# Attention and GELU on one core: transfers of 4096 tokens, fewer gelu and check instructions, the last batch stored by unit, and a second pass 11 units behind

## The chip, the cores and the metric

The kernel runs on one core of one Trainium2 chip. The metric is the device time of one execution in microseconds (us). Runs are fast or slow. Engines: PE is TensorE (PEld its weight loads), DVE VectorE, ACT ScalarE, POOL GpSimd, SP SyncE. "Granted clock" is the share of full TensorE speed that the throttle allowed.

## The reference

```python
B, N, m, C = 4, 12480, 32, 128               # x is [B, N, C] float32, d_ff = 2048
h   = softmax(scale * inducing @ x.T) @ x    # first pass: 32 rows per batch, needs all of x
out = softmax(scale * x @ h.T) @ h           # second pass: every token of x again
out = gelu(out @ w_in) @ w_out               # gelu(t) = 0.5 t (1 + erf(t / sqrt 2))
```

The output of the attention is a weighted mean of 32 rows `h` per batch. For the given inputs the kernel therefore takes the MLP of those 32 rows only, q = MLP(h), and mixes q in the second pass. It approximates gelu by a quadratic, tests on the chip that the inputs allow all this, and would otherwise branch to a general path.

Every float32 of x is read once (25.56 MB), every output is written once (25.56 MB), and the weights are 2.1 MB.

## The kernel before

A batch has six units of 2048 tokens and a tail of 192. The first pass takes, per unit: load with a cast to fp16, transposes, scores, exp, and a sum `hun` on PE. After the seventh unit a chain of small steps makes h and q:

```python
# chain(): one step waits for the one before it
hun_out (ACT), r1_sum (DVE), h_sum (PE), h_out (DVE), up (PE, 16 matmuls), up_out (ACT)
# gelu in four steps: three long instructions of DVE and two short ones
nc.vector.tensor_reduce(out=bt.hs, in_=bt.pt, axis=AX.X, op=ALU.add)
# ... slope and offs from hs ...
nc.vector.tensor_tensor(out=bt.sl, in0=bt.pt, in1=slope, op=ALU.mult)
nc.vector.tensor_tensor(out=bt.gl, in0=bt.sl, in1=offs, op=ALU.subtract)
down (PE), down_out (ACT), q_sum (PE), q_out (DVE)
# later, off the chain: squares of pt and their sums on DVE, judged batch by batch
```

The second pass scores each unit against h, mixes q (`at`, in PSUM), scales by 1/sum into `o`, and stores `o`. One of four parts is copied by ACT and scaled by POOL, always the same one; the others go to DVE or ACT.

```python
XBUFS = 11     # input buffers of one unit
BEHIND = 14    # the second pass stands this many units behind the first in the order
AWAY = (0,)    # the part that goes by ACT and POOL
...            # six output buffers "o" of one unit, one store of 1 MB per unit, on SP's queue
```

A small planner in the kernel fixes the order of instructions of each engine before the kernel is built, from assumed durations. On the chip the order is fixed: an engine that waits for one instruction runs nothing behind it (experiment 2 shows such a wait, of 4.49 us).

## Time and profile before

| | before |
|---|---|
| median of 3 runs | 136.24 us (136.13 to 136.53) |
| span of the profiled run | 133.9 us, clock 0.892 |
| HBM traffic | 27.67 MB read, 25.56 MB written |
| busy: PE, DVE, ACT, POOL | 75, 74, 65, 32% |
| last chain hun_sb (starts at 101.0 us) to the start of q | 10.0 us |

The page of the kernel before: span; slices of 1/40 of the span (granted clock and DMA share in tenths, then GB/s); packets; queues (packets, MB, share of 16 engines).

```profile
span 133.9 us, 3622 instructions
...
PEclk9999999559999999999959999996899965799755
DMA  3999999999999999999999999999999989989993
GB/s 98 322 210 215 213 213 202 214 217 215 214 210 212 273 281 290 291 307 296 322 313 312 322 252 314 318 373 412 423 422 425 423 374 421 379 340 418 428 404 110
DMA packets 8547, 40.18 MB, mean 300 GB/s; under 512 B 944, under 2 KB 2256, under 8 KB 5328
...
q0 software_dynamic: 4432, 13.31, 50.6%
q1 hardware_dynamic: 4096, 26.63, 49.0%
q8 instruction: 11, 0.18, 0.5%
...
HBM read 27.67 MB, written 25.56 MB: 397 GB/s over the span
```

DMA is at 9 nearly everywhere from the second slice on, and the two data queues fill 99.6% of 16 engines' span (50.6 + 49.0; packets can overlap, so in a stretch the share can pass 1, as in the table below). The GB/s row counts a cast load at its fp16 size, so 213 there is 426 GB/s of reading. Everything is hidden behind the transfers except where the row falls in the last third: 374, 379 and 340, between 107 and 121 us.

Busy microseconds by stretch in the kernel before (windows view; the last two columns are DMA share and GB/s):

```profile
core 0: us, PE busy (x) PEld busy (x) DVE busy (x) ACT busy (x) POOL busy (x), PEclk, DMA share, GB/s
20.00:40.00 20.00, 15.81 (x277) 10.87 (x275) 13.52 (x34) 11.30 (x26) 4.98 (x9) 0.83 1.09 212
45.00:93.00 48.00, 42.64 (x615) 25.12 (x613) 43.48 (x115) 37.70 (x99) 15.27 (x17) 0.95 1.04 313
...
105.00:123.00 18.00, 13.62 (x94) 5.08 (x93) 16.17 (x43) 13.76 (x42) 6.74 (x7) 0.81 0.94 388
123.00:129.00 6.00, 1.86 (x14) 0.74 (x14) 2.59 (x11) 2.81 (x9) 1.13 (x2) 0.71 1.02 423
129.00:134.00 5.00, 0.00 (x0) 0.00 (x0) 0.00 (x0) 0.00 (x0) 0.00 (x0) 0.50 0.54 202
```

The stretch from 105 to 123 us holds only stores and moves 388 GB/s where 424 is to be had. DVE is 90% busy there and the clock is 0.81. This is the time in which batch 3, the last, runs its chain and begins its second pass. I call this the hole.

Three instructions of the chain (tile view of `pt`: engine, operation, count, then nanoseconds min/median/max and first and last start):

```profile
L448 ACT ACTIVATE pt<-pt_ps x4: 597/610/626, 28.5 to 104.3; 128x512 f32<-128x512 f32 x4
L452 DVE TENSOR_REDUCE hs<-pt x4: 669/686/689, 29.2 to 105.0; 128x16 f32<-128x512 f32 x4
L476 DVE TENSOR_TENSOR sl<-pt,slope x4: 691/692/1495, 30.1 to 105.9; 128x512 f32<-128x512 f32 x4
```

`sl` usually takes 0.69 us but 1.495 us at 105.9 us, in the last batch.

### The profile page before, as it was taken

The numbers are of one execution on the slowest core, as the hardware profiler recorded it, in microseconds if no ns is written. First come the engines' busy times: TensorE is split into PE (matmuls) and PEld (weight loads), VectorE is DVE, ScalarE is ACT, GpSimd is POOL, SyncE is SP. The second block draws the span as 40 slices with busy tenths as digits, with TensorE's granted clock in tenths as the row PEclk, the third lists the DMA queues.
The fourth block names the chain that finished last, engine by engine and source line by source line (L and its number), as shares of the span: only waits on it lengthen the run. The fifth ranks groups of instructions, "written<-read, shape, count | busy, mean of one in ns | idle before, by whom it ended". The sixth has DMA issues, their size and how long they took to land.

```text
span 133.9 us, 3622 instructions
## 1 busy us (share of the span) xinstructions
PE 100.9 (75%) x1371; PEld 58.3 (44%) x1371; DVE 99.2 (74%) x290; ACT 86.9 (65%) x222; POOL 42.3 (32%) x59
## 2 busy tenths in 40 slices
PE   0299773599999998999689898996968859883400
PEld 0147561466666564656276364451635333231100
DVE  1068434259899989999986998996699998895700
ACT  3006865049577789998916977658668964879600
POOL 6911331112153402345403216113333601445300
PEclk9999999559999999999959999996899965799755
DMA  3999999999999999999999999999999989989993
GB/s 98 322 210 215 213 213 202 214 217 215 214 210 212 273 281 290 291 307 296 322 313 312 322 252 314 318 373 412 423 422 425 423 374 421 379 340 418 428 404 110
DMA packets 8547, 40.18 MB, mean 300 GB/s; under 512 B 944, under 2 KB 2256, under 8 KB 5328
## 3 DMA queue, kind: packets, MB, share of 16 engines
q0 software_dynamic: 4432, 13.31, 50.6%
q1 hardware_dynamic: 4096, 26.63, 49.0%
q8 instruction: 11, 0.18, 0.5%
q14 instruction: 8, 0.07, 0.1%
HBM read 27.67 MB, written 25.56 MB: 397 GB/s over the span
## 4 chain that ended last, share of the span: by engine, by line
DMA 58%; PE 16%; ACT 7%; DVE 7%; issue 4%; POOL 3%; POOLq 0%; DVEq 0%; ACTq 0%; SPq 0%
DMA xh<-in_x_dram 46%; DMA out_dram<-o 13%; PE at L661 7%; DVE o L698 4%; ACT o L691 3%; PE tr L330 2%; PE s L618 2%; POOL xh L240 2%; ACT e L630 1%; PE hun L378 1%; ACT o L313 1%; DVE sl L476 1%; PE r L642 1%; DVE hs L452 1%; PE q_ps L510 0%
## 5 line engine op out<-in xcount | busy, mean ns | idle before, releaser
L683 POOL TENSOR_TENSOR o<-o,rr 128x512 f32<-128x512 f32 x24 | 25.5, 1065 | 43.9 <-ACT o L313 31.2
L661 PE MATMUL at<-q,e 128*128 128x512 f16 (+1 forms) x104 | 34.3, 392 | 5.5 <-ACT o L313 1.8
L698 DVE TENSOR_TENSOR o<-at,rr 128x512 f32<-128x512 f32 (+1 forms) x57 | 35.2, 642 | 2.6 <-issue 0.7
L330 PE MATMUL tr<-identity_h,xh 128*128 128x128 f16 x392 | 29.3, 228 | 4.3 <-DMA xh<-in_x_dram 3.6
L330 PEld LDWEIGHTS <-xh 128*128 128x128 f16 x392 | 24.2, 102 | 10.6 <-DMA xh<-in_x_dram 5.3
L311 DVE COPY xT<-tr 128x1024 f16<-128x1024 f16 (+1 forms) x34 | 21.2, 641 | 9.0 <-PE tr L330 8.7
L240 POOL DMA_DIRECT2D xh<-in_x_dram x27 | 14.8, 551 | 39.4 <-DMA xh<-in_x_dram 13.0
L313 ACT ACTIVATE xT<-tr 128x1024 f16<-128x1024 f16 (+1 forms) x18 | 17.6, 990 | 11.4 <-PE tr L330 11.3
L691 ACT ACTIVATE o<-at,rr 128x128 f32<-128x128 f32 (+1 forms) x83 | 23.6, 371 | 2.1 <-PE at L661 1.9
L356 ACT ACTIVATE e<-s 128x512 f16<-128x512 f32 (+1 forms) x28 | 15.2, 543 | 8.2 <-PE s L344 6.6
L630 ACT ACTIVATE e<-s 128x512 f16<-128x512 f32 (+1 forms) x28 | 15.0, 558 | 4.3 <-PE at L661 2.2
L313 ACT ACTIVATE o<-at 128x512 f32<-128x512 f32 x24 | 14.5, 605 | 2.7 <-DMA out_dram<-o 1.3
L661 PEld LDWEIGHTS <-e 128*128 128x128 f16 (+1 forms) x104 | 9.0, 103 | 14.1 <-issue 9.6
L378 PE MATMUL hun<-xh,e1t 128*32 128x128 f16 x392 | 11.1, 233 | 3.9 <-DVE e1t L370 3.9
L370 DVE STREAM_TRANSPOSE e1t<-e 128x256 int32<-128x256 int32 (+1 forms) x28 | 10.9, 397 | 1.9 <-ACT e L356 1.5
L344 PE MATMUL s<-xT,indT 128*32 128x512 f16 (+1 forms) x108 | 10.0, 366 | 1.4 <-ACT xT L313 0.8
L618 PE MATMUL s<-xT,hT 128*32 128x512 f16 (+1 forms) x100 | 11.0, 442 | 0.0
L378 PEld LDWEIGHTS <-e1t 128*32 128x32 f16 x392 | 6.4, 100 | 7.5 <-DVE e1t L370 5.1
L642 PEld LDWEIGHTS <-e 128*128 128x128 f16 (+1 forms) x104 | 5.7, 101 | 7.9 <-ACT e L630 3.2
L642 PE MATMUL r<-strand,e 128*128 128x4 f16 (+1 forms) x104 | 6.6, 169 | 2.1 <-ACT e L630 1.7
L653 DVE RECIPROCAL rr<-r 128x16 f32<-128x16 f32 (+1 forms) x28 | 5.7, 224 | 1.6 <-PE r L642 1.6
L344 PEld LDWEIGHTS <-indT 128*32 128x32 f16 x108 | 3.5, 93 | 6.0 <-issue 3.6
(69 smaller groups left out, 80.4 us busy)
## 6 DMA issues: line engine op xcount, KB each, us to landing
out_dram<-o SPq DMA_DIRECT2D x24, 1024.0 KB, 9.4
xh<-in_x_dram POOLq DMA_DIRECT2D x23, 512.0 KB, 18.6
x_first<-in_x_dram SPq DMA_DIRECT2D x1, 1024.0 KB, 5.0
w_in_h<-in_moe_w_in_dram POOLq DMA_DIRECT2D x1, 512.0 KB, 16.8
w_out_h<-in_moe_w_out_dram POOLq DMA_DIRECT2D x1, 512.0 KB, 18.8
out_dram<-o SPq DMA_DIRECT2D x4, 96.0 KB, 8.9
xh<-in_x_dram POOLq DMA_DIRECT2D x4, 48.0 KB, 20.2
ind_s<-in_inducing_dram SPq DMA_DIRECT2D x1, 16.0 KB, 4.7
```

The lines of the kernel that those rows point to most:

```text
L240: nc.gpsimd.dma_start(out=xh[: u.p, : u.nc, :], in_=src)
L311: nc.vector.tensor_copy(out=out, in_=in_)
L313: nc.scalar.activation(out=out, in_=in_, func=AF.Copy)
L330: nc.tensor.transpose(tr[:, c - c0, : u.p], xh[: u.p, c, :], identity_h[: u.p, : u.p])
L356: nc.scalar.activation(out=e1[: u.p, : u.nc // 2, :, :], in_=s1[: u.p, : u.nc, :].rearrange("r (a b) i -> r a i b", b=2), func=AF.Exp, sca ...
L378: nc.tensor.matmul(bt.hun[32 * j : 32 * j + 32, :], e1t[: u.p, c // 2, :, c % 2], xh[: u.p, c, :], start=u.idx == 0 and c < 4, stop=c + 4 ...
L618: nc.tensor.matmul(s2[32 * j : 32 * j + 32, : u.cols], bt.hT, bt.xT_of(u, j * u.nci, (j + 1) * u.nci), start=True, stop=True,)
L630: nc.scalar.activation(out=e2[: u.rows, : u.cols], in_=s2[: u.rows, : u.cols], func=AF.Exp, scale=SCALE,)
L661: nc.tensor.matmul(at[: u.p, : u.nj, :], e2[: u.rows, ci * u.p : (ci + 1) * u.p], bt.q[: u.rows, : u.nj, :], start=True, stop=True,)
L683: nc.gpsimd.tensor_tensor(out=part, in0=part, in1=rr2[: u.p, ci, : u.nj].unsqueeze(2).broadcast_to([u.p, u.nj, 128]), op=ALU.mult,)
L691: nc.scalar.activation(out=ov[: u.p, ci, j, :], in_=at[: u.p, j, :], func=AF.Copy, scale=rr2[: u.p, ci, j : j + 1],)
L698: nc.vector.tensor_tensor(out=ov[: u.p, ci, :, :], in0=at[: u.p, : u.nj, :], in1=rr2[: u.p, ci, : u.nj].unsqueeze(2).broadcast_to([u.p, u. ...
```

## The change

Its intent: fewer and larger transfers, a shorter chain, less work on DVE, and a last batch whose outputs need no output buffer. Core of the diff, with cuts:

```diff
-XBUFS = 11
-BEHIND = 14
-AWAY = (0,)
+XBUFS = 6                      # buffers of two units
+OBUFS = 3                      # buffers of two units
+BEHIND = 11
+APART = 3                      # from this batch on: store by unit
...
+            xh = sb.tile([128, 32, 128], FP16, tag="xh", bufs=XBUFS)   # one load of 2 MB
...
-        (gelu_sum, gelu_line, gelu_mult, gelu_out)
+            nc.vector.scalar_tensor_tensor(out=bt.gl, in0=z, scalar=0.5 / CGELU,
+                in1=z, op0=ALU.add, op1=ALU.mult)          # CGELU goes into strand_c, for q
...
-            nc.vector.tensor_tensor(out=bt.zsq, in0=bt.pt, in1=bt.pt, op=ALU.mult)
-            nc.vector.tensor_reduce(out=bt.ssq, in_=bt.zsq, axis=AX.X, op=ALU.add)
+            nc.gpsimd.tensor_tensor(...)     # squares, then five halving additions on POOL
+        # one total and one judgement at the end, for all four batches
...
+        elif u.b >= APART:                   # last batch: the output lies in an input buffer
+            o = sb.tile([128, 32, 128], FP16, tag="xh", bufs=XBUFS)
+            o = o.rearrange("p c d -> p (c d)").bitcast(FP32)
...
-            if ci in AWAY and not u.tail:    # ACT copies, POOL scales
+                    {"DVE": 0.1 + 0.57 * u.nj / 4, "ACT": 0.285 * u.nj}
+                    | ({} if u.tail else {"ACT+POOL": 0.6}),    # the planner chooses
```

## The prediction

> **What bounds it now.** The DMA engines. The slice row has DMA at 9 nearly throughout from 3 us on; the queue part adds to 100% of 16 engines. HBM moves 53.2 MB. Counting a load at its 4-byte source size, the trace's packets run at 420 to 427 GB/s in the load-only stage (6 to 40 us), about 417 in the mixed stage, about 424 in store-only stretches. Against 424 GB/s, the span of 133.9 us loses about: 2.7 us before the pipe is full, 0.45 us at 42 to 45 us, 0.9 us over the mixed stage, 1.5 us between 105 and 121 us, 0.6 us in the last 3 us of transfer, 1.5 us after the last byte. PE, DVE and ACT are 65 to 75% busy and hidden, except in the hole at 105 to 121 us: there the chain of waits is compute. Batch 3's chain runs from hun_sb at 101.0 to q at 111.7; its units follow with PE 0.89 busy at a granted clock of 0.74 (windows view).
>
> **What the change does.**
> 1. Transfers of 4096 tokens double the run per partition (16 KB of HBM). Packet durations (59 ns for 512, 98 for 1024, 324 for 4096 bytes of fp16) fit about 0.0735 ns a byte plus some 20 ns, mostly overlapped. The Trainium skill, "DMA: Bandwidth & Descriptors", "Why small descriptors are slow", names a fixed cost per packet; this trace agrees. The slope alone is 435 GB/s, today 424, so halving the packets is worth at most half the gap, 1.3% of 50 MB: 0.8 to 1.5 us, on the critical path everywhere. Stores may gain less.
> 2. The gelu part of the chain (hs, slope, sl, gl: 105.0 to 108.1 us, 3.1 us) becomes one DVE operation of about 0.7 us: 2.4 us less latency. It counts only in batch 3.
> 3. DVE loses about 3.6 us a batch (gelu 1.7, squares and sum 1.36, judging 0.5), 14 of 99 us. POOL gains about 3.4 us of checks a batch and 13 more scalings at 1.07 us (order of instructions: 37 against 24). Only the 2 to 3 us of DVE after 105 us touch the hole.
> 4. With 11 units behind, stores begin about 3 units sooner, but only when a pair is done; fewer units of batch 2 remain to cover batch 3's chain (4 to 5, some 11 us of DMA, against about 8 us of chain plus 3 us for the first unit). About neutral.
> 5. Pairs make buffers come free in lumps (6 for loads, 3 for stores): new DMA gaps, 0.2 to 0.8 us.
>
> **Sum.** -1.1 (packets), -0.9 (hole), -0.3 (42 to 45), -0.2 (mixed stage), +0.4 (lumps): about -2.1 us. The floor, 53.2 MB at 430 GB/s plus fill and end, is about 129.5 us of span, 4.4 us less. Predicted time 134.1 us, 8 in 10 between 132.2 and 135.8. Faster by over 2%: 0.38; within 2%: 0.57; slower by over 2%: 0.05.
>
> **How the profile would show it.** Load packets of twice the bytes at under twice the time; load-only slices nearer 216 than 213 GB/s; no slice below 400 GB/s after the last load; DVE near 85 us; POOL near 60; batch 3's hun_sb to q about 8 us; first store near 36 to 38 us.
>
> **What would make it wrong.** Packets split at the old size, so no rate gain; lumpy buffers starving loads around 40 to 60 us, or stores during batch 3's chain; POOL's scalings and checks holding back the loads behind them in its order; or the hole closing wholly and both directions reaching 430, which would give about 132.

## The result

| | before | changed |
|---|---|---|
| median | 136.3 us (136.13 to 136.53, 4 runs) | 134.72 us (134.16 to 134.78, 4 runs) |
| ratio of fast runs | | 0.9874 (95%: 0.9844 to 0.9904): faster, but by less than 2% |
| span of the profile | 133.9 us | 132.8 us |
| PE, DVE, ACT, POOL busy, us | 100.9, 99.2, 86.9, 42.3 | 97.3, 93.4, 76.2, 65.3 |

A ratio is the mean time of one kernel's fast runs over that of the other's of the same rounds, so it is not quite the ratio of the medians. In five rounds the changed kernel had 134.21 us and 0.9898 (0.9829 to 0.9966). They were run at other times.

The page of the changed kernel, the same lines:

```profile
span 132.8 us, 3490 instructions
...
PEclk9999999965899999999999999999999999955555
DMA  4999999999999999999999999999999999999970
GB/s 123 302 223 215 217 200 220 212 220 210 220 205 220 215 200 313 333 398 367 299 318 348 266 227 324 321 412 425 430 423 426 415 437 413 411 434 425 421 300 15
DMA packets 5666, 40.17 MB, mean 303 GB/s; under 512 B 624, under 2 KB 1936, under 8 KB 2192
...
q0 software_dynamic: 2848, 13.30, 49.5%
q1 hardware_dynamic: 2800, 26.63, 48.3%
q8 instruction: 11, 0.18, 0.5%
...
HBM read 27.67 MB, written 25.56 MB: 401 GB/s over the span
```

Packets fell from 8547 to 5666. The dips of the last third are gone: from the slice with 412 on, no slice is below 411 until the last two. But those end badly: 300 and 15, where before had 404 and 110.

Stretches of the changed kernel (same columns as before):

```profile
20.00:40.00 20.00, 15.79 (x257) 11.15 (x254) 11.37 (x30) 9.88 (x22) 7.28 (x12) 0.83 1.08 216
51.00:93.00 42.00, 36.48 (x571) 21.79 (x570) 35.65 (x100) 31.41 (x69) 24.35 (x29) 1.00 1.02 335
...
105.00:123.00 18.00, 12.82 (x91) 5.17 (x91) 16.28 (x55) 10.40 (x27) 13.14 (x15) 0.81 1.00 424
123.00:126.00 3.00, 0.00 (x0) 0.00 (x0) 0.00 (x0) 0.00 (x0) 0.00 (x0) 0.50 0.99 410
126.00:132.00 6.00, 0.00 (x0) 0.00 (x0) 0.00 (x0) 0.00 (x0) 0.00 (x0) 0.50 0.46 185
```

The load-only stretch moves 216 instead of 212, the stretch of the hole 424 instead of 388. Then DMA share falls to 0.46 in the last six microseconds, in which no engine computes.

Part of the changed chain (tile view of `pt`), where L562 is the halving additions and L491 the new gelu:

```profile
L562 POOL TENSOR_TENSOR pt<-pt x20: 244/458/1279, 31.2 to 110.1; 128x512 f32<-128x512 f32 x4, 128x256 f32<-128x256 f32 x4, 128x128 f32<-128x128 f32 x4, 128x64 f32<-128x64 f32 x4
L485 ACT ACTIVATE pt<-pt_ps x4: 597/597/597, 27.6 to 103.3; 128x512 f32<-128x512 f32 x4
L491 DVE SCALAR_TENSOR_TENSOR gl<-pt x4: 693/754/985, 28.3 to 104.1; 128x512 f16<-128x512 f32 x4
```

Gelu takes 0.75 us in the median. From the start of hun_sb (100.6 us) to the start of q (106.4 us) is now 5.8 us, against 10.0 before.

### Where the time went

To compare stretches I count what was lost: the length of a stretch, less the bytes that the trace's packets moved in it (loads at their float32 size) divided by 424 GB/s, a rate that store-only stretches of both kernels reach. "End" is when the last data packet ended.

| profile | lost 0 to 93 us | lost 93 to 126 us (hole) | lost 126 us to end | lost after 93 us | end |
|---|---|---|---|---|---|
| before | 4.27 | 1.55 | 1.00 | 2.55 | 132.38 |
| changed | 3.14 | -0.04 | 2.51 | 2.47 | 131.16 |

So 1.1 us were gained by 93 us, as packets went faster, and the hole of 1.6 us closed. Yet 1.5 us of that came back at the very end. The landings say why. A transfer is split over 16 DMA engines, and each signals when its share is done. The Trainium skill, "DMA: Bandwidth & Descriptors", section "Why a DMA increments its semaphore by 16 and not by 1", says that these engines finish independently and that only all 16 signals mean that the data has landed. This trace agrees, with numbers. These are the first, median and last of the 16 signals of some stores, worked out from the trace's records of semaphores (us):

```
store issued at      first    median   last
before  104.05       108.81   109.90   111.36      issued before the hole
before  110.07       115.07   115.33   116.21      issued in the hole
before  119.97       123.98   124.08   124.19      after the hole
before  126.86       131.98   132.09   132.84      the last store
changed 112.40       117.73   118.82   120.50
changed 120.54       125.10   126.18   128.07
changed 122.60       127.98   129.09   131.62      the last store
```

In the changed kernel the first of 16 engines runs about 3 us ahead of the last, and nothing ever lets the last one catch up. In the kernel before, the hole does: the fast engines stand idle in it while the slow ones work off their queues, and the spread falls from 2.5 to 1.1 and then to 0.2 us. The kernel ends with its slowest engine: the span ends 1.08 us (before) and 1.14 us (changed) after the last of these signals.

### The profile page after: what moved, and what is told of

It is laid out like the page before. It is cut to its first block, busy times and chain, and to the rows that moved or that the text cites. A ratio compares the mean times of both kernels' runs of the same rounds, so it can differ in the third digit from the quotient of the medians.

```text
span 132.8 us, 3490 instructions
## 1 busy us (share of the span) xinstructions
PE 97.3 (73%) x1365; PEld 56.6 (43%) x1365; DVE 93.4 (70%) x266; ACT 76.2 (57%) x173; POOL 65.3 (49%) x85
## 5 line engine op out<-in xcount | busy, mean ns | idle before, releaser
L686 POOL TENSOR_TENSOR pair<-pair,rr 128x512 f32<-128x512 f32 x29 | 30.3, 1056 | 29.1 <-ACT pair L355 19.9
L670 PE MATMUL at<-q,e 128*128 128x512 f16 (+1 forms) x104 | 33.5, 389 | 7.2 <-DVE o L701 2.4
L701 DVE TENSOR_TENSOR pair<-at,rr 128x512 f32<-128x512 f32 x41 | 26.8, 679 | 3.1 <-DMA out_dram<-pair 1.6
L355 ACT ACTIVATE xT<-tr 128x1024 f16<-128x1024 f16 (+1 forms) x17 | 16.7, 981 | 19.1 <-PE tr L367 19.1
L355 ACT ACTIVATE pair<-at 128x512 f32<-128x512 f32 x29 | 17.2, 598 | 3.1 <-PE at L670 1.7
L277 POOL DMA_DIRECT2D xh<-in_x_dram x15 | 8.3, 556 | 21.5 <-DMA xh<-in_x_dram 14.3
L562 POOL TENSOR_TENSOR pt<-pt 128x512 f32<-128x512 f32 (+4 forms) x20 | 12.0, 601 | 1.5
L701 DVE TENSOR_TENSOR o<-at,rr 128x512 f32<-128x512 f32 (+1 forms) x19 | 10.2, 558 | 0.9 <-PE at L670 0.7
L686 POOL TENSOR_TENSOR o<-o,rr 128x512 f32<-128x512 f32 x8 | 8.2, 1044 | 4.0 <-ACT o L355 2.3
L616 PE MATMUL s<-xT,hT 128*32 128x512 f16 (+1 forms) x100 | 9.7, 391 | 0.1
```

Source lines behind the costliest of these rows:

```text
L355: nc.scalar.activation(out=out, in_=in_, func=AF.Copy)
L562: nc.gpsimd.tensor_tensor(out=bt.pt[:, :, :, :half], in0=bt.pt[:, :, :, :half], in1=bt.pt[:, :, :, half : 2 * half], op=ALU.add,)
L670: nc.tensor.matmul(at[: u.p, : u.nj, :], e2[: u.rows, ci * u.p : (ci + 1) * u.p], bt.q[: u.rows, : u.nj, :], start=True, stop=True,)
L686: nc.gpsimd.tensor_tensor(out=part, in0=part, in1=rr2[: u.p, ci, : u.nj].unsqueeze(2).broadcast_to([u.p, u.nj, 128]), op=ALU.mult,)
L701: nc.vector.tensor_tensor(out=ov[: u.p, ci, :, :], in0=at[: u.p, : u.nj, :], in1=rr2[: u.p, ci, : u.nj].unsqueeze(2).broadcast_to([u.p, u. ...
```

## The experiments

I call "theory A" that the time ends with the slowest DMA engine, so that a hole shorter than the lag between engines costs it nothing. "Theory B" is that the hole counts in full, and that the spread at the end was an accident. The 12 runs follow. In these experiments the runs of the kernel before, slow ones included, varied between 134.6 and 138.91 us, and the intervals of the ratios reach 0.6 to 1.2% to either side. So differences under about 1% are not told apart by time, and I lean on profiles there.

### 1. The changed kernel again (after_again)

> The changed kernel once more, as the yardstick of this call. Both theories: 0.985 to 0.990 of before. By theory A (the last store ends when the slowest of the 16 DMA engines ends, and an idle hole shorter than the lag between engines is free for that engine) the landings of the last stores are again spread over 2.5 to 4 us from the first engine to the last; by theory B (the spread at the end was an accident of one profile) over less than 1.5 us.

134.21 us (133.88 to 134.72), ratio 0.9898. Its profile had a hole of 0.96 us after all, at 102 to 117 us, yet it ended earlier than the first one, at 130.25 us: the last store's landings spread from 129.99 to 130.86 us. So the spread expected by A did not come, because there was a hole. A hole of one microsecond that costs nothing is what A says. The spread is not fixed to the kernel, though: A as I worded it for this run missed, and what B said (under 1.5 us) came.

### 2. Each half of the change alone (old_steps, small, old_gelu)

old_steps: large transfers, 11 units, last batch by unit, but gelu, checks and fixed scaling as before (the judging at the end for all batches was kept). The edit, in words:

```diff
-            gelu in one instruction; squares and sums on POOL; ACT+POOL where the planner likes
+            hs, slope, offs, sl, gl; squares and sums on DVE; part 0 alone by ACT and POOL
```

> Transfers of 4096 tokens, the last batch by unit and 11 units of lag, with the gelu, checks (on VectorE) and fixed scaling of before. If the larger transfers are what pays: 1.0 to 1.5 us faster than before (0.989 to 0.993) although a hole of 1 to 2 us in the last batch's stores is there. If the steps are what pays: within 0.4 us of before.

133.92 us (133.78 to 134.87), ratio 0.9879 (0.9808 to 0.9949), against 0.9898 of the changed kernel. Without any of the new steps the whole gain is there. Hole 0.58 us, end of the last data packet 129.94 us, last signal 131.25 us.

small: the new steps with the sizes of before.

```diff
-XBUFS = 6; OBUFS = 3; BEHIND = 11; APART = 3
+XBUFS = 11; OBUFS = 6; BEHIND = 14; APART = 4    # tiles of one unit, one transfer per unit
```

> The new gelu, check and scaling steps with the transfers, buffers and 14 units of lag of before. My estimate: the hole at 105 to 121 us closes as in the changed kernel, the rate of transfers stays as before. Theory A: the end spread is then over 2.5 us and the time is within 0.5 us of before (0.996 to 1.004). Theory B: about 1.4 us faster than before (0.990).

142.52 us, ratio 1.0492 (1.0396 to 1.0589): slower, which neither theory had. The page:

```profile
DMA  3999999999999999999999999999999960579991
GB/s 121 310 209 213 205 212 219 211 211 207 218 214 211 232 314 361 316 313 313 325 304 304 278 315 312 383 418 421 425 414 430 423 259 0 222 301 411 428 421 54
```

A slice with 0 GB/s stands where the last batch should be stored; its hun_sb came at 110.7 us instead of 101.0. Its timeline from 37 us on, first DVE, then POOL (start, length, what, and idle time before it with the releaser):

```profile
37.59 0.43 DVE L407 STREAM_TRANSPOSE e1t<-e 128x256 int32<-128x256 int32 x1
42.51 0.19 DVE L576 SCALAR_TENSOR_TENSOR left<-pt 128x16 f32<-128x16 f32 x1 [4.49 <-POOL pt L562]
```

```profile
36.99 1.04 POOL L277 DMA_DIRECT2D xh<-in_x_dram  x2 [1.94 <-PE tr L367]
38.05 1.05 POOL L551 TENSOR_TENSOR pt<-pt 128x512 f32<-128x512 f32 x1
39.18 3.30 POOL L562 TENSOR_TENSOR pt<-pt 128x512 f32<-128x512 f32 x5
```

DVE stood idle 4.49 us for the last of POOL's halving additions. POOL's check had started only at 38.05 us because a load's issue stood ahead of it in POOL's order, and that had waited 1.94 us for the transposes that free its buffer. In the changed kernel the same check starts at 30.0 us, and DVE waits for it 0.2 us in all.

old_gelu: the changed kernel with the four-step gelu only.

> The changed kernel with the old four-step gelu on VectorE, so that the last batch's chain is about 2.4 us longer and VectorE does 1.7 us more a batch. Theory A: a hole of at most 1 us appears in the stores at 107 to 114 us, the spread between DMA engines shrinks by as much, and the time is within 0.4 us of the changed kernel. Theory B (a shorter chain pays its full length once the transfers are the limit): 1 to 2.4 us slower than the changed kernel.

137.11 us, in two groups: 134.92 to 135.83 in the four fast runs and 138.39 to 140.48 in the four slow ones. Ratio of the fast ones 0.9954 (0.9863 to 1.0045), that is about 0.75 us over the changed kernel by the two ratios and 1.0 us by the plain means of the fast runs (135.28 and 134.28 us), with an interval that does not exclude either theory. The profile fell on a slow run, so I draw nothing from it.

### 3. The lag, and the last batch by unit (small11, before11, behind14, apart4)

Having first blamed the order of the passes for experiment "small", I changed the lag alone in three kernels:

```diff
-BEHIND = 14      # small -> small11; before -> before11
+BEHIND = 11
-BEHIND = 11      # changed -> behind14
+BEHIND = 14
```

> The new steps with transfers of 2048 tokens, now 11 units behind. Theory C (in the run with 14 units the last batch's first pass stood in the fixed order of each engine behind second-pass work that waits for store buffers, so its hun_sb came at 110.7 us): with 11 units hun_sb of the last batch comes at 100 to 104 us again, the hole of 8 us at 114 to 123 us is gone and the time is 0.99 to 1.003 of before, the rest of the gain of the changed kernel being the rate of the larger transfers. If the 2048-token buffers themselves are the trouble: again over 1.03.

142.93 us, 1.0539: "theory C" fell. The lag is not what ails that kernel.

> The kernel before with its second pass 11 units behind, nothing else changed. If the lag is what pays: 1 to 1.5 us faster than before. If the larger transfers pay, or if only a hole of 1.5 us is closed that the slower DMA engines do not feel: within 0.5 us of before (0.996 to 1.004).

137.09 us, 1.0089 (0.9995 to 1.0182): not faster. Its loads of x end at 99.6 us instead of 93.0, since earlier stores take their share; its hole is 2.94 us.

> The changed kernel with its second pass 14 units behind again. Theory C: the last batch's first pass comes late, hun_sb after 105 us, a hole of 3 us or more in the stores, and 2 to 6 us slower than the changed kernel. If the lag is neutral, as the prediction had it: within 0.5 us of the changed kernel, 0.985 to 0.993 of before.

134.94 us (133.98 to 136.0), 0.9919 (0.9823 to 1.0015): nothing that can be told from the changed kernel, as the prediction had it.

```diff
-APART = 3        # changed -> apart4: the last batch too is stored in pairs, from output buffers
+APART = 4
```

> The changed kernel with the last batch stored in pairs too, from the output buffers. If storing by unit pays: the first store of the last batch starts 2 to 3 us later, a hole of 1 to 3 us opens before it, and by theory A (the slower DMA engines do not feel a hole shorter than their lag) only 0 to 1.5 us of it reach the time. If it does not matter: within 0.4 us of the changed kernel.

136.74 us (136.56 to 139.11), 1.007 (0.9953 to 1.0187): about 1.7% over the changed kernel, so the whole gain and more is lost.

```profile
DMA  4999999999999999999999999999999997979990
GB/s 127 302 226 212 219 192 222 219 214 217 212 217 207 224 231 319 333 394 366 295 329 331 229 282 314 333 421 424 421 431 424 409 441 288 403 302 438 370 382 17
```

The first store of the last batch was issued at 113.9 us (changed: 111.4) and the next ones at 119.9 and 124.4 us, in steps of two units. The slices 288, 302 and 370 are the holes between, 2.36 us in all. A store of a pair waits for its second unit; in this stretch the stores have no work in hand to hide that.

### 4. Where the small kernel's loss came from (small_dvecheck)

```diff
-        p = stage(key, "POOL", 1.1, check_square, [p_gelu])
-        p = stage(key, "POOL", 2.4, check_sum, [p])
+        p = stage(key, "DVE", 1.3, check_square, [p_gelu, bt.made_q])
+        p = stage(key, "DVE", 0.7, check_sum, [p])
```

> The new gelu and scaling with transfers of 2048 tokens and 14 units of lag, but the squares and their sums back on VectorE. Theory D (in the run with 2048-token transfers GpSimd issues a load only when the load eight before it has landed, so the checks behind it in its fixed order come late, and VectorE, which needs their sum next in its own order, stood idle 4.5 us at 38 to 42.5 us and again in each batch): the wait of VectorE for GpSimd's sum is gone, hun_sb of the last batch comes before 105 us and the time is 0.985 to 1.005 of before. If the checks are not the cause: again over 1.03.

135.43 us (134.54 to 136.89), 0.9964 (0.9856 to 1.0071). The loss is gone, hun_sb of the last batch comes at 101.9 us, and no wait of DVE for POOL's sums is left. So it was the checks on POOL, tied to DVE by the fixed order. One detail of my wording was off: at the stall I looked at, POOL had waited for a free input buffer, not for a landing.

```profile
DMA  4999999999999999999999999999999999999970
GB/s 115 314 210 213 216 209 206 216 215 215 207 218 194 306 262 276 348 319 231 329 313 295 270 315 325 309 383 419 419 422 429 424 427 426 425 429 422 419 319 17
```

This run tells more. It has transfers of 2048 tokens and no hole at all: no slice after the last load is under 419 until the end. And it gains next to nothing: the loss of the hole moved to its end (319 and 17). Its last store's signals run from 129.10 to 132.56 us.

### 5. A hole put in on purpose (delay6, delay12)

```diff
             nc.scalar.activation(out=bt.qp, in_=bt.qp_ps, func=AF.Copy)
+            if b == B - 1:
+                for _ in range(6):            # delay12: 12
+                    nc.scalar.activation(out=bt.qp, in_=bt.qp, func=AF.Copy)
```

> The changed kernel with six extra copies in the last batch's chain on ScalarE, about 2 us. Theory A (the end is set by the slowest DMA engine, and a hole in the stores shorter than the lag between engines costs nothing): the hole before the last batch's stores is at most 1 us on average over the engines, the spread of the last landings shrinks, and the time is within 0.4 us of the changed kernel (0.986 to 0.994 of before). Theory B: the hole is added to the time in full.

136.62 us (135.5 to 137.61), 1.0108 (1.0002 to 1.0215); fast runs 135.5 and 135.69. I expected at most 0.4 us more than the changed kernel and got 1.3 us and more, so A failed in its number. (The edit also told the planner of the copies, so the order of other instructions may differ a little.) In its profile the hole was 1.13 us. Up to the next-to-last store the slowest engine was not late by it (128.38 us, against 128.31 and 128.13 us in the two profiles of the changed kernel); then the last 1 MB took it 3.9 us, against 3.3 and 2.7. In that time (129.88 us) there is an instruction fetch of 0.88 us on the DMA engines; below I come back to it.

> The same with twelve copies, about 4 us. Theory A: a hole of 2 to 4 us on average over the engines, the last landings spread over less than 1 us, and the time longer than the changed kernel by the hole less 1 to 2 us. Theory B: longer by the whole hole.

138.47 us, 1.0258 (1.0156 to 1.0361).

```profile
DMA  5999999999999999999999999999999994499991
GB/s 130 297 222 219 207 200 229 205 224 207 208 226 205 227 215 326 360 387 317 311 342 321 233 273 316 374 429 434 413 431 424 422 434 164 183 408 412 424 417 46
```

The hole is 4.00 us (slices 164 and 183). The profiled run is about 3.1 to 3.9 us longer in span (135.9) than those of the changed kernel (132.8 and 132.0), and the other timed runs are longer still. The lag is gone in the hole: the first store after it, issued at 116.7 us, landed from 120.44 to 120.63 us on all 16. For a hole of 4.0 us A had said 2 to 3 us more time than the changed kernel, and B 4.0. The spans lie between, and the medians, which are of different calls, differ by 4.3 us. So A had the landings right, but its number missed in both runs with a hole put in on purpose.

Together, profile by profile, as in the first table. Rows are sorted by the hole; old_gelu and behind14 are left out, for their profiles are of slow runs, and so are the two small kernels with a long stall:

| profile | tokens | lost 0 to 93 | hole | lost 126 to end | lost after 93 | end | last signal | lost 93 to last signal |
|---|---|---|---|---|---|---|---|---|
| changed | 4096 | 3.14 | -0.04 | 2.51 | 2.47 | 131.16 | 131.62 | 2.92 |
| small_dvecheck | 2048 | 4.01 | 0.08 | 2.47 | 2.55 | 132.12 | 132.56 | 3.00 |
| old_steps | 4096 | 3.00 | 0.58 | 0.81 | 1.38 | 129.94 | 131.25 | 2.69 |
| warm_old (see 6) | 4096 | 3.08 | 0.86 | 0.71 | 1.57 | 130.36 | 131.54 | 2.74 |
| after_again | 4096 | 3.11 | 0.96 | 0.62 | 1.58 | 130.25 | 130.86 | 2.19 |
| delay6 | 4096 | 3.15 | 1.13 | 1.93 | 3.07 | 131.77 | 132.25 | 3.55 |
| before | 2048 | 4.27 | 1.55 | 1.00 | 2.55 | 132.38 | 132.84 | 3.01 |
| apart4 | 4096 | 3.16 | 2.36 | 1.73 | 4.09 | 132.80 | 133.30 | 4.59 |
| before11 | 2048 | 4.28 | 2.94 | 0.97 | 3.92 | 133.76 | 134.42 | 4.58 |
| delay12 | 4096 | 3.23 | 4.00 | 0.96 | 4.96 | 133.75 | 134.73 | 5.94 |

The span ended 1.08 to 1.14 us after the last signal (apart4: 1.32), while the last signal came 0.4 to 1.3 us after the last data packet. So time follows the signal, and the last column counts to it. That loss shows no trend while the hole is under about 1.6 us: 2.2 to 3.0, and 3.55 in delay6. Beyond that it grows: 4.6 at holes of 2.4 and 2.9 us, 5.9 at 4.0 us. The scatter among the short holes, 2.19 to 3.55 us, I cannot predict; each row is one execution.

Part of the scatter goes with the last instruction fetch, of 0.88 to 1.0 us. In changed, small_dvecheck, delay6, old_steps and apart4 it began 1.4 to 3.6 us before the last signal, and in the store that landed last the sixteenth signal came 0.78 to 1.22 us after the fifteenth. In before, after_again and before11 it began only 0.6 to 0.8 us before the last signal, and the sixteenth came 0.05 to 0.20 us after the fifteenth (warm_old and delay12 lie between in both). No run moved the fetch, so this is a coincidence in time, not a shown cause; it is a rival to the hole for part of what the end costs.

### 6. The dip at the first store (warm_old)

In each of the ten profiles of the table there is a microsecond, just when the first large store begins, in which load packets take about twice their time (at most 807 ns instead of 324 before, 1276 instead of 625 in the changed kernel); 0.35 to 0.55 us are lost (48 to 51 us in the kernels with transfers of 4096 tokens, 42 to 45 us in the others). I added one small early store to old_steps:

```diff
     nc.sync.dma_start(out=ind_s, in_=inducing)
+    nc.sync.dma_start(out=out[0:128, :], in_=identity)    # overwritten later
```

> The kernel with the old steps and the 4096-token transfers, with one 64 KB store to the output added in the first microseconds (overwritten later). If the dip at the first store (0.35 to 0.46 us in every profile, packets of loads that take twice their time) is the first touch of the output in HBM: the dip at 48 to 51 us is gone and the time is about 0.3 us shorter than without, 0.983 to 0.988 of before. If it comes with the first large store itself: the dip stays.

134.3 us, 0.9914 (0.9855 to 0.9974), and the dip is the same (0.36 us against 0.35 us). It is not cured by a first touch of those 64 KB. What it is stays open. No version that I tried is clearly faster than the changed kernel.

### What makes one engine late

In both kernels all 16 engines land within 1.1 us at first. The first large lag comes with the transfer that is in flight when the first instruction block is fetched (queue 8, 16384 bytes, 0.96 us, at 18.9 us): in the kernel before, the load that ended next landed from 20.28 to 20.81 us on 15 engines and at 21.90 us on the last. After the second and the third fetch (27.5 and 36.7 us) one more engine each was about 1 us late. In the changed kernel, whose engines were 1.1 us apart from the start, such steps are less plain. The Trainium skill, "Runtime: NRT & Kernel Launch", section "Instruction fetch mechanics", has blocks of 16 KiB that the sequencers fetch by DMA; the traces agree, with 11 such packets in each kernel. The coincidence in time is clear, but I made no run with fewer fetches, so the cause of the lag is argued from traces, not shown by an experiment; nor do these traces say which of the 16 engines is the late one, so that some engine is slower by itself is not excluded.

## Why the prediction was right or wrong

The time, 134.1 us with a range of 132.2 to 135.8, held 134.72 us, and "within 2%" was right. Its steps:

- **DMA bounds the kernel; at most a few microseconds are to be had.** Right.
- **Packets, -1.1 us.** Right in size, less so in place. The Trainium skill, "DMA: Bandwidth & Descriptors", section "Why small descriptors are slow", names a fixed cost per packet, of about 3 cycles, and finds joining worth it only for descriptors of up to 256 bytes. The trace agrees that there is a fixed part, but here it still paid with packets of kilobytes: in the median a load packet of twice the bytes took 625 ns where two took 648, a store packet 611 where two took 618. By 93 us the changed kernel had lost 3.14 us instead of 4.27. The prediction counted -1.1 and -0.2 for this; measured -1.1. But it had the gain everywhere. From 6 to 40 us, with loads alone, the loss fell from 0.22 to -0.05 us; from 51 to 93 us, with loads and stores mixed, from 0.80 to 0.07; from 93 to 105 us, with stores alone, it did not fall (0.02 and 0.04). It goes with the size of transfers in every profile: from 51 to 93 us the five profiles with 2048 tokens lost 0.65 to 0.81 us, the nine with 4096 lost 0.03 to 0.24. Small_dvecheck against the changed kernel says it again: neither has a hole, their ends have the same loss, and they differ by 0.96 us in their end.
- **Hole, -0.9 us.** Mis-sized, and the term that was missing stands next to it. The hole closed wholly (-1.6 us), but the end lost +1.5 us, as the slow DMA engines no longer had a pause to catch up in. What the hole was worth was about 0.1 us between these two profiles (2.55 and 2.47 us lost after 93 us). The prediction measured the hole as the mean of 16 engines, and the end is set by the last of them.
- **Gelu shorter by 2.4 us, of use in batch 3.** The chain got shorter by more than that (10.0 to 5.8 us), but old_steps has the old gelu and all of the gain. So with large transfers it brought no time that these runs can tell; whether it makes the kernel steadier, as the slow runs of old_gelu hint, stays open.
- **DVE down by 14 us, to about 85.** Wrong: 93.4 us. DVE took 60 of the scaled parts (57 before), as the planner now chooses, which is about 2 us. The small check instructions that stayed on DVE (the lines of `left` and `quart`) took 7.9 us instead of 3.7, one of them 540 ns in the mean where its like took 174 before. Neither was in the sum. POOL came to 65 us, not 60. Neither cost time in this kernel. Small shows that the checks on POOL can cost 6 us and more where POOL's order is unlucky; "POOL's checks holding back the loads" was the feared direction, and the reverse happened.
- **42 to 45 us, -0.3.** Wrong: the dip moved to 48 to 51 us and kept its size (0.45 us before, 0.46 after).
- **First store near 36 to 38 us.** Wrong: 45.6 us. It needs two finished units, and PE was 97% busy from 40 to 50 us.
- **11 units behind: about neutral.** Right for the changed kernel (behind14), and no gain for the kernel before (before11).
- **Lumps, +0.4.** Not seen in the mixed stage. They would have come at the end: apart4 loses 2.3 us. That the last batch is stored by unit is what avoids them.

Sum: -1.2 us of span measured against -2.1 predicted; -1.1 is packets. Of the other terms the -0.9 and the -0.3 did not come, nor did the +0.4, so the packets alone carry the forecast; that the time still fell in the range owes something to a range 3.6 us wide.

One more difference shows only over many runs. In the calls after the first, fast runs of the kernel before lay between 134.6 and 136.66 us, those of the changed kernel between 133.88 and 134.72 us. The three fastest of the kernel before, 134.6 to 134.79 us, had a granted clock of 0.923 to 0.931, while the changed kernel had 134.07 us at 0.886. This fits a hole that grows when PE is slow and a kernel that has little (0.96 us in after_again) or none to grow. It is a correlation: no run set the clock.

## What to carry to other kernels

When DMA engines are full, as here, the end is the slowest engine's, so price an idle stretch by what that engine loses in it. In these profiles holes of up to about 1.6 us cost nothing that stands out of the scatter, and closing one gained nothing; but the two runs with a hole put in on purpose cost more than that reading said, so it is argued more than shown. Larger transfers paid here while loads ran, most where loads and stores mixed, but only with small ones left at the end, where a store waits for its last unit. And moving work to an idle engine ties its fixed order to those that need the result: check what stands ahead of it there.

## What the Trainium skill lacked or had wrong

- "Runtime: NRT & Kernel Launch", "Instruction fetch mechanics", calls the cost of crossing a 16 KiB block "mostly hidden". It lacks that the fetch occupies a DMA engine that carries data: 11 packets, mostly 0.88 to 1.04 us each, and in the kernel before one more engine about 1 us late after each of the first three (cause argued, see above).
- "DMA: Bandwidth & Descriptors" says that the 16 engines finish independently, but gives no size for how far apart. Here the first and last of them were 2.6 to 3.6 us apart in the back-to-back stores at the end of the changed kernel, and 0.2 us apart after a hole of 4 us.
- No page has the dip at the first large store: 0.35 to 0.55 us lost while load packets take about twice their time, not changed by an early store of 64 KB.
